# Other orders of moving words in the products of zeros at the head of a recurrence and expert kernel

## The chip, the cores and the metric

The kernel runs on one core of a Trainium2 chip. The metric is device time in microseconds (us); lower is better. The kernel before takes 1058.9 us, the median of three runs (1058.42, 1058.90 and 1058.95).

Engines go by the profile's names: PE is TensorE's matrix products and PEld its loads of held operands (the words that stay in the array while the moving words stream past), DVE is VectorE, ACT is ScalarE, POOL is GpSimd. SP issues most DMAs. L817 is line 817 of the kernel.

## The reference

A gated linear recurrence over 768 steps for 4 batches and 8 heads of 48 values, and then a mixture of 4 experts on the 3072 rows of 384 values that it gives:

```python
for t in range(S):
    state = alpha[:, :, t, :, None] * state + np.einsum('bhd,bhe->bhde', k[:, :, t], v[:, :, t])
    y[:, :, t] = np.einsum('bhd,bhde->bhe', q[:, :, t], state)
x = y.transpose(0, 2, 1, 3).reshape(B * S, H * D)
p = domain_probs / (domain_probs.sum(-1, keepdims=True) + 1e-09)
for e in range(E):
    h = np.maximum(x @ w1[e], 0.0)
    out += p[:, e:e + 1] * (h @ w2[e])
```

Everything is float32. `w1` is 4 x 384 x 1024, `w2` is 4 x 1024 x 384.

## The kernel before

The recurrence is cut into 24 units: one unit is 128 time steps of one batch, all 8 heads. `attention(u)` is a generator; each `next` on it emits one step of one unit's work. The first three steps transpose the unit's alpha, k and q on TensorE (tile tp, L277), and copy or multiply them out of PSUM (L288, L293, L307). Then follow seven levels of doubling (m = 1, 2, 4, ... 64): at each level ScalarE copies every second stretch of m words of q (`copy_q`, qb, L328), VectorE multiplies decays into q and k (`next_q` L335 and L337, `next_k` L348), and TensorE makes the scores (sc, L355; the last level is far, L410). VectorE takes the scores in through masks (`take`, L365), ScalarE and VectorE gather them in lat (L423, L428), and TensorE makes the result (yps, L450), which ScalarE copies into the experts' input xT (L467).

The experts are `up` (the first layer, tiles one and two, L562 and L570) and `down` (the second, tile ops, L663). They go over groups of units: a first group of two, and then groups of four. The first group's first unit, 128 rows, goes through the first expert alone, as soon as its result is there, while the second unit is still on its way.

The order of the work on each engine is the order in which the program emits it (`manual_schedule`); an engine runs its instructions in that order, each one when its operands are there. At the head, which lasts some 30 us, a list written out by hand interleaves steps of units 0 and 1 with products of zeros:

```python
for u, n in ((0, 3), (0, 3), (0, 1), (0, 1), (0, 1), (0, 1), (0, 1), (1, 0), (0, 0), (0, 1),
             (0, 1), (1, 1), (0, 1), (1, 0), (0, 0), (0, 2), (0, 2), (0, 0)):
    next(runs[u])
    (fill if n > 2 else single)(n)
```

After a step of unit `u`, `fill(3)` emits three products of zeros of 128 columns (L798), and `single(n)` emits `n` turns of six products of zeros of 384 columns (L817). The results go to a PSUM tile `idle` that nothing reads; the operands come from `nothing`, a tile of 2304 words a partition that VectorE sets to zero (L794). It is one of the buffers of the first layer's weights, and is free until those need it. Its type is float32r, as that of the experts' products.

There are 13 turns, taken in order from the list `turns`. Turns 1 to 5 stand ahead of the transposes of unit 1's alpha, 6 and 7 ahead of those of its k, 8 and 9 ahead of those of its q, and 10 to 13 ahead of unit 0's result (yps). In the kernel before, a turn is given by four numbers: the step between held words, the step between moving words (negative: backwards), the number of held columns, and where in the tile the moving words begin.

Loads are issued by SP in the order in which they are emitted: inputs of units 0 and 1, the probabilities, four pieces of the first expert's first layer (L221, L222), unit 2's alpha, k and q (L174), and the first expert's second layer (L224).

Of the kernel before, what the change touches and what calls it, by code (L numbers as in the profile page):

```python
# [20 lines left out]
def kernel(  # L21
# [37 lines left out]
    nc = tc.nc  # L59

    B, H, S, D = q.shape
    E, DM, F = moe_w1.shape
    P = 128
# [21 lines left out]
    n = np.arange(QUAD)[None, :]  # L85
# [81 lines left out]
    def load(u, names):  # L167
        if u >= len(units):
            return
        cb, b = units[u]  # L170
        for nm in names:
            src = srcs[nm][b, :, cb * P:(cb + 1) * P, :].rearrange("h s d -> s h d")
            if nm != "v":
                nc.sync.dma_start(out=raw(u, nm)[:, :, :D], in_=src)  # L174
                continue

            pairs = raw(u, nm).rearrange("p (a i) d -> p a i d", i=2)
            src = src.rearrange("p (a i) d -> p a i d", i=2)
            nc.sync.dma_start(out=pairs[:, :, 0, :D], in_=src[:, :, 0])
            nc.sync.dma_start(out=pairs[:, :, 1, :TAIL], in_=src[:, :, 1, QUAD:])  # L180
            nc.sync.dma_start(out=pairs[:, :, 1, TAIL:D], in_=src[:, :, 1, :QUAD])
# [13 lines left out]
    def load_piece(l, i, beside=False):  # L195
        if i >= E * NQ * LAST:
            return
        gi, k = divmod(i, E * NQ)
        e, c = divmod(k, NQ)
        if gi > l:  # L200
            w = wt[l][i] = wts.tile([P, 3, KC * QF], F32R, name=f"w{l + 1}",
                                    bufs=AHEAD if l == 0 else NQ)
            nc.sync.dma_start(out=w.bitcast(F32), in_=kept[l][k])
            return
        if l == 1 and not beside:
            return
        if l == 0:

            if gi > 0 or e == 0:
                shared[c] = wts.tile([P, 3, KC * QF], F32R, name="w2", bufs=NQ)  # L210
            w = shared[c][:, 2 - e % 2 if gi == 0 else 2].bitcast(F32)
        else:

            place = (hidden[c][:, 0] if not split2(gi, e, c) else hidden[c + NQ // 2][:, 1])
            w = place.rearrange("p f n -> p (f n)")[:, :KC * QF].bitcast(F32)
        wt[l][i] = w
        if l == 0:
            heads = moe_w1[e].rearrange("(h d) f -> h d f", d=D)[:, :, c * QF:(c + 1) * QF]
            w = w.rearrange("p (c f) -> p c f", f=QF)
            for part in range(2):  # L220
                nc.sync.dma_start(out=w[:, part], in_=heads[part * H // 2:(part + 1) * H // 2, :QUAD])  # L221
            nc.sync.dma_start(out=w[:, 2], in_=heads[:, QUAD:])  # L222
        else:
            nc.sync.dma_start(  # L224
                out=w.rearrange("p (c d) -> p c d", d=DM),
                in_=moe_w2[e].rearrange("(c p) d -> p c d", p=P)[:, c * FPQ:(c + 1) * FPQ])
# [36 lines left out]
    def norm_probs():  # L263
        nc.vector.reduce_sum(out=tot, in_=p_all, axis=AX.X)
        nc.vector.tensor_scalar_add(out=tot, in0=tot, scalar1=1e-9)
        nc.vector.reciprocal(out=tot, in_=tot)
        nc.vector.tensor_mul(p_all, p_all, tot.unsqueeze(2).broadcast_to([P, NBLK, E]))
        nc.vector.tensor_scalar_mul(out=p_fine, in0=p_all, scalar1=FINE)
# [439 lines left out]
    def cost(layer, gi, e):  # L708
        n = len(groups[gi]) / 4
        if layer == 0:  # L710
            return 2.1 * n if split1(gi, e) else 2.6 * n
        return 4.1 if gi > 1 else 4.7 if split2(gi, e) else 5.4
# [50 lines left out]
    def advance(spent):  # L763
        nonlocal clock
        clock += spent
        while waiting and clock >= waiting[0][0]:
            next(waiting.popleft()[2], None)

    with tc.manual_schedule():
        nc.scalar.dma_start(out=ident_all, in_=nc.inline_tensor(ident_np, name="ident_c").ap())  # L770
        nc.scalar.dma_start(out=masks, in_=nc.inline_tensor(mask_np, name="masks_c").ap())
        nc.gpsimd.memset(sts[B - 1], 0.0)
        for nm in "akq":
            for r in (early[nm], apart[nm]):
                nc.gpsimd.memset(r[:, :, D:], 0.0)
        nc.gpsimd.memset(lat[HALF:, :, :HALF], 0.0)
        for t in values + blocks:
            nc.gpsimd.memset(t, 0.0)
        for t in sts[:-1]:
            nc.gpsimd.memset(t, 0.0)  # L780

        load(0, "akqv")
        load(1, "akqv")
        nc.sync.dma_start(out=p_all, in_=moe_domain_probs.rearrange("(n p) e -> p n e", p=P))
        for i in range(NQ):
            load_piece(0, i)

        idle = ps.tile([P, NT], F32, name="idle", tag="g", bufs=4)  # L790
        zeros = sts[B - 1].rearrange("p a i d -> p (a i d)")[:, :P]
        nothing = wts.tile([P, 3, KC * QF], F32R, name="w1", bufs=AHEAD)
        nothing = nothing.rearrange("p t n -> p (t n)")
        nc.vector.memset(nothing.bitcast(F32), 0.0)  # L794

        def fill(n):
            for _ in range(n):
                nc.tensor.matmul(idle[:, :P], lhsT=zeros, rhs=zeros, start=True, stop=True)  # L798

        def words(n, at):  # L800
            return nothing[:, at:at + n]

        def turn(held=1, moving=1, m=P, away=16):
            return held, moving, m, away

        turns = deque([turn(), turn(2), turn(2, -1), turn(4), turn(4, -1), turn(m=66), turn(1, -1),
                       turn(2, -1, away=12), turn(3), turn(3, -1), turn(1, 2), turn(1, away=20), turn(2, 2)])

        def stepped(n, at, step):
            span = words(n * abs(step), at)[:, ::abs(step)]  # L810
            return span if step > 0 else span[:, ::-1]

        def single(n):
            for _ in range(n):
                held, moving, m, away = turns.popleft()
                for i in range(6):
                    nc.tensor.matmul(idle[:m, :DM], lhsT=stepped(m, 512 * (i % 2), held),  # L817
                                     rhs=stepped(DM, 1024 + away, moving), start=True, stop=True)

        runs = [attention(u) for u in range(len(groups[0]))]  # L820
        fill(7)
# [4 lines that stand above are left out]
        norm_probs()  # L826

        span = cost(0, 0, 0) * FCH / 2 + cost(1, 0, 0)
        waiting.extend((span * (k + 1) / 15, u, runs[u])
                       for k, u in enumerate([1, 1, 1, 0, 1, 0, *[1] * 8]))  # L830
        for fc in range(FCH):
            up(0, 0, fc, slice(0, 1))
            advance(cost(0, 0, 0) / 2)
        down(0, 0, [0], deque())
        while waiting:
            next(waiting.popleft()[2], None)
        clock = 0.0
        waiting.extend((1.0 + k, 1, runs[1]) for k in range(2))
        waiting.extend(deal())

        for (gi, e), after in zip(tasks, [*tasks[1:], (None, None)]):
            rest = gi == e == 0
            for fc in range(FCH):
                up(gi, e, fc, slice(1, len(groups[0])) if rest else None)
                advance(cost(0, gi, e) / (2 if rest else 1))
            each = len(groups[gi]) if split2(gi, e) else 1
            turns = [range(k, k + each) for k in range(rest, len(groups[gi]), each)]
            for k, slots in enumerate(turns):

                between = deque()  # L850
                if after[1] == 0:

                    for step, at in enumerate((0.0, 0.3, 0.42, 0.54) if gi == 0 else
                                              (0.0, 0.6, 0.7, 0.78)):
                        at = at * len(turns) - k
                        if 0 <= at < 1:
                            between.append((at, lambda step=step: split_x(after[0], step)))
                down(gi, e, slots, between)
        while stores:
            stores.popleft()()  # L860
# [28 lines left out]
```

## Time and profile before

| | us |
|---|---|
| median of three runs | 1058.9 |
| the profiled execution | 1059.26 |
| its span, first to last instruction | 1057.4 |
| PE busy (98% of the span) | 1041.3 |
| DVE busy (74%) | 780.9 |
| ACT busy (53%) | 565.7 |
| PE busy in the 78 products of zeros at L817, between 8.15 and 30.03 | 17.5 |

A product's duration in the profile is longer than its share of TensorE's time, because products overlap: one of 384 columns is recorded with some 340 ns, and the next one begins some 174 ns after it. So where the pace matters, the distance from start to start is taken, or a window's length divided by the products in it. In the timeline, instructions of one line that follow each other are put together, with their count; idle time ahead of a row and what ended it stand in brackets.

### The profile page before, as it was taken

How to read it: one execution, taken by the hardware profiler on the slowest of the kernel's cores; microseconds unless marked ns; L12 is line 12 of the kernel's file. 1: busy time of each engine (PE TensorE's matmuls, PEld its weight loads, DVE VectorE, ACT ScalarE, POOL GpSimd, SP SyncE). 2: the span in 40 equal slices, each digit the busy share in tenths (PEclk: the TensorE clock that was granted, in tenths of full speed). 3: DMA queues.
4: the chain of work that ended last, by engine and by line, in shares of the span. 5: the costliest groups of instructions: out<-in, count | busy, mean ns of one | idle time of the engine just before them, and what ended most of it. 6: DMA issues, size and time to landing. Idle time of an engine off the chain costs nothing.

```text
span 1057.4 us, 21736 instructions
## 1 busy us (share of the span) xinstructions
PE 1041.3 (98%) x8560; PEld 905.3 (86%) x8560; DVE 780.9 (74%) x1621; ACT 565.7 (53%) x1195; POOL 37.7 (4%) x81
## 2 busy tenths in 40 slices
PE   9899999999999999999999999999999999999998
PEld 8676777677878798898998998998989889898998
DVE  6477868668778968777877777986978776656565
ACT  4588866664767546446555435555464543323232
POOL 3000000000000100000000000000000000000000
PEclk9999999999999999999999999999999999999999
DMA  7496889897877949568679569586594454444531
GB/s 118 138 301 187 287 264 363 324 349 256 277 254 246 384 133 374 213 211 325 222 231 330 176 256 338 179 304 236 166 370 177 197 209 167 192 179 179 201 158 45
DMA packets 158550, 251.68 MB, mean 238 GB/s; under 512 B 120144, under 2 KB 134864, under 8 KB 135920
## 3 DMA queue, kind: packets, MB, share of 16 engines
q1 hardware_dynamic: 151984, 207.89, 58.4%
q0 software_dynamic: 6016, 42.08, 10.0%
q8 instruction: 68, 1.11, 0.4%
q10 hardware_dynamic: 448, 0.32, 0.1%
q14 instruction: 34, 0.28, 0.1%
HBM read 207.79 MB, written 42.47 MB: 237 GB/s over the span
## 4 chain that ended last, share of the span: by engine, by line
PE 86%; DVE 5%; ACT 5%; DMA 2%; issue 1%; SPq 0%; POOL 0%; ACTq 0%; DVEq 0%; POOLq 0%
PE ops L663 35%; PE one L570 23%; PE two L570 11%; PE sc L355 6%; PE tp L277 3%; PE yps L450 3%; ACT qb L328 2%; PE idle L817 2%; PE one L562 2%; DMA hT<-in_moe_w_dram 1%; PE sps L489 1%; PE far L410 1%; DVE hT L616 1%; DVE near L365 1%; DMA rq<-in_q_dram 1%
## 5 line engine op out<-in xcount | busy, mean ns | idle before, releaser
L663 PE MATMUL ops<-w,hT 128*128 128x384 f32 x1872 | 342.7, 340 | 0.2 <-DVE hT L616 0.2
L663 PEld LDWEIGHTS ops<-w,hT 128*128 128x128 f32 x1872 | 322.6, 188 | 4.0 <-ACT t L581 0.6
L570 PE MATMUL one<-xT,w 128*128 128x512 f32 x960 | 251.9, 398 | 0.4 <-ACT t L581 0.4
L570 PEld LDWEIGHTS one<-xT,w 128*128 128x128 f32 x960 | 176.3, 188 | 38.2 <-ACT t L581 1.2
L581 ACT ACTIVATE t<-one 128x512 f32<-128x512 f32 (+1 forms) x192 | 106.8, 556 | 175.0 <-PE one L570 169.8
L328 ACT COPY qb<-QT 64x256 f32<-64x256 f32 x336 | 136.6, 407 | 58.2 <-DVE QT L335 29.9
L610 DVE SCALAR_TENSOR_TENSOR hT<-t,hT 128x512 fp32r<-128x512 f32 (+1 forms) x172 | 110.4, 642 | 63.3 <-ACT hT L608 62.1
L583 DVE TENSOR_TENSOR t<-t,two 128x512 f32<-128x512 f32 (+1 forms) x172 | 109.3, 635 | 53.2 <-PE two L570 31.7
L608 ACT ACTIVATE hT<-t 128x512 fp32r<-128x512 f32 (+1 forms) x172 | 101.8, 592 | 86.8 <-DVE t L583 86.3
L570 PE MATMUL two<-xT,w 128*128 128x512 f32 x480 | 136.5, 393 | 0.1
L570 PEld LDWEIGHTS two<-xT,w 128*128 128x128 f32 x480 | 90.1, 188 | 20.4 <-DVE acc L692 0.9
L663 PE MATMUL ops<-hT 128*128 128x384 f32 x288 | 100.8, 492 | 0.5 <-DMA hT<-in_moe_w_dram 0.4
L616 DVE SCALAR_TENSOR_TENSOR hT<-hT 128x512 fp32r<-128x512 f32 (+1 forms) x172 | 100.7, 635 | 0.0
L365 DVE COPY_PREDICATED near<-masks,sc 128x256 f32<-128x256 uint8 x144 | 77.1, 536 | 23.3 <-PE sc L355 20.4
L335 DVE TENSOR_TENSOR QT<-QT,dec 128x256 f32<-128x256 f32 x144 | 61.1, 424 | 39.2 <-ACT qb L328 38.6
L355 PEld LDWEIGHTS sc<-qb,KT 128*64 128x64 f32 x2304 | 72.7, 138 | 9.0 <-issue 4.4
L355 PE MATMUL sc<-qb,KT 128*64 128x64 f32 x2304 | 77.2, 223 | 2.6 <-ACT qb L328 2.6
L663 PEld LDWEIGHTS ops<-hT 128*128 128x128 f32 x288 | 52.1, 190 | 30.3 <-DMA hT<-in_moe_w_dram 1.0
L692 DVE SCALAR_TENSOR_TENSOR acc<-ops,p_all,acc 128x384 f32<-128x384 f32 x82 | 49.8, 614 | 27.1 <-PE ops L663 26.3
L348 DVE TENSOR_TENSOR KT<-KT,dec 128x256 f32<-128x256 f32 x144 | 60.3, 419 | 0.0
L347 ACT COPY KT<-KT 128x256 f32<-128x256 f32 x138 | 57.5, 416 | 5.1 <-PE sc L355 1.9
L562 PE MATMUL one<-xT,w 128*128 128x256 f32 (+1 forms) x240 | 46.2, 340 | 0.6 <-ACT xT L467 0.6
(93 smaller groups left out, 949.1 us busy)
## 6 DMA issues: line engine op xcount, KB each, us to landing
w<-kept SPq DMA_DIRECT2D x144, 1152.0 KB
kept<-w POOLq DMA_DIRECT2D x32, 1152.0 KB, 6.9
hT<-in_moe_w_dram SPq DMA_DIRECT2D x32, 384.0 KB
w<-in_moe_w_dram SPq DMA_DIRECT2D x48, 128.0 KB
ra<-in_alpha_dram SPq DMA_DIRECT2D x23, 192.0 KB
rk<-in_k_dram SPq DMA_DIRECT2D x23, 192.0 KB
rq<-in_q_dram SPq DMA_DIRECT2D x23, 192.0 KB
out_dram<-acc POOLq DMA_DIRECT2D x22, 192.0 KB, 6.8
```

Source lines behind the costliest of these rows:

```text
L328: nc.scalar.copy(out=qb[rows, :, i, :].rearrange("p a (b r) -> p a b r", r=m), in_=qv[rows])
L335: nc.vector.tensor_mul(qv, qv, spread(dv[:, :, :, 0], m))
L355: nc.tensor.matmul(out[HALF * s:HALF * (s + 1), 2 * p:2 * p + 2, :], lhsT=KTs[li][:, p, HALF * s:HALF * (s + 1)], rhs=qbs[li][:, p, :, QUA ...
L365: nc.vector.copy_predicated(near.rearrange("p a (b two r) -> p a b two r", two=2, r=m)[:, :, :, 1, :], mk.unsqueeze(1).broadcast_to([P, H, ...
L562: nc.tensor.matmul(one, lhsT=w[:, kc], rhs=xraws[gi][:, kc, lo:hi], start=(kc == 0), stop=(kc == KC - 1))
L570: nc.tensor.matmul(out, lhsT=w[:, part, kc], rhs=x_part(gi, part, kc), start=(part == terms[0] and kc == 0), stop=(part == terms[-1] and k ...
L581: nc.scalar.activation(out=t, in_=one, func=ACT.Copy, scale=FINE)
L583: nc.vector.tensor_add(t, t, two)
L608: nc.scalar.activation(out=top, in_=x, func=ACT.Relu, scale=TRIM)
L610: nc.vector.scalar_tensor_tensor(out=low, in0=x, scalar=0.0, in1=top.bitcast(F32), op0=ALU.max, op1=ALU.subtract)
L616: nc.vector.scalar_tensor_tensor(out=dif, in0=top.bitcast(F32), scalar=1 / 4096.0, in1=low.bitcast(F32), op0=ALU.mult, op1=ALU.subtract)
L663: nc.tensor.matmul(sums[at], lhsT=h, rhs=w, start=(n == begins[at]), stop=(n == ends[at]))
```

## The change

The list of turns is replaced. There are still 13 turns of six products, at the same places, with 384 moving columns each. The held words are now always 128 neighbours. The moving words all begin at word 1040 of the tile. Turn 1 reads 384 neighbours. Turns 2 to 6 read a stretch of 8, 16, 32, 64 and 128 words over and over, turn 7 one of 192 words twice. Turns 8 to 13 read groups of four neighbouring words (a line of 16 bytes): `every(k, n)` takes n groups, each the first of k, and goes over them until 384 words are read. So turns 8 to 11 take every second, fourth, eighth and sixteenth group, turn 12 every third and turn 13 every sixth.

```diff
-        def turn(held=1, moving=1, m=P, away=16):
-            return held, moving, m, away
-
-        turns = deque([turn(), turn(2), turn(2, -1), turn(4), turn(4, -1), turn(m=66), turn(1, -1),
-                       turn(2, -1, away=12), turn(3), turn(3, -1), turn(1, 2), turn(1, away=20), turn(2, 2)])
-
-        def stepped(n, at, step):
-            span = words(n * abs(step), at)[:, ::abs(step)]
-            return span if step > 0 else span[:, ::-1]
+        def again(n):
+            return words(n, 1040).unsqueeze(1).broadcast_to([P, DM // n, n])
+
+        def every(k, n):
+            lines = words(4 * k * n, 1040).rearrange("p (n w) -> p n w", w=4 * k)[:, :, :4]
+            return lines.unsqueeze(1).broadcast_to([P, DM // (4 * n), n, 4])
+
+        turns = deque([words(DM, 1040), *(again(8 << i) for i in range(5)), again(192),
+                       every(2, 48), every(4, 48), every(8, 24), every(16, 12), every(3, 48), every(6, 48)])
 
         def single(n):
             for _ in range(n):
-                held, moving, m, away = turns.popleft()
+                moving = turns.popleft()
                 for i in range(6):
-                    nc.tensor.matmul(idle[:m, :DM], lhsT=stepped(m, 512 * (i % 2), held),
-                                     rhs=stepped(DM, 1024 + away, moving), start=True, stop=True)
+                    nc.tensor.matmul(idle[:, :DM], lhsT=words(P, 512 * (i % 2)), rhs=moving, start=True, stop=True)
```

`words(n, at)` is a stretch of n words of `nothing`.

## The prediction

> **What bounds the kernel now.** I read the page first, for the engine that carries the span; then TensorE's timeline over the first 32 us, where every changed product lies; then the busy time stretch by stretch there; last ScalarE's timeline, for what the products hide. The page:
>
> ```profile
> span 1057.4 us, 21736 instructions
> PE 1041.3 (98%) x8560; PEld 905.3 (86%) x8560; DVE 780.9 (74%) x1621; ACT 565.7 (53%) x1195; POOL 37.7 (4%) x81
> PE ops L663 35%; PE one L570 23%; PE two L570 11%; PE sc L355 6%; PE tp L277 3%; PE yps L450 3%; ACT qb L328 2%; PE idle L817 2%; PE one L562 2%; DMA hT<-in_moe_w_dram 1%; PE sps L489 1%; PE far L410 1%; DVE hT L616 1%; DVE near L365 1%; DMA rq<-in_q_dram 1%
> ```
>
> TensorE is busy 98% of the span, and the products of zeros (idle, L817) hold 2% of the chain that ended last. So they are on the path, and are not filler for a wait. TensorE's timeline says where:
>
> ```profile
> 8.16 6.19 PE L817 MATMUL idle<-w 128*128 128x384 f32 x30
> 14.19 0.60 PE L277 MATMUL tp<-ident,hT 128*128 128x128 f32 x4
> 14.72 2.09 PE L355 MATMUL sc<-qb,KT 128*64 128x64 f32 x64
> 16.73 2.32 PE L817 MATMUL idle<-w 128*66 128x384 f32 x12
> 18.89 0.60 PE L277 MATMUL tp<-ident,hT 128*128 128x128 f32 x4
> 19.24 2.38 PE L817 MATMUL idle<-w 128*128 128x384 f32 x12
> ...
> 23.51 6.59 PE L817 MATMUL idle<-w 128*128 128x384 f32 x24
> 30.03 1.08 PE L450 MATMUL yps<-lat,rv 128*32 128x128 f32 x32
> 31.71 3.62 PE L562 MATMUL one<-xT,w 128*128 128x128 f32 x30 [0.60 <-ACT xT L467]
> ```
>
> Columns: start, length, engine, line, count, and idle time before. From 8.16 to 31.11 us no row has idle time: each real step stands behind a run of zero products, and moves when they get longer or shorter. The same stretches by turn (six products each), L817 alone; the counts include a neighbour that reaches over an edge:
>
> ```profile
> 8.15:11.38 3.23, 3.22 (x18) 3.23 (x19) 1.00 1.54 161
> 11.38:14.19 2.81, 2.81 (x13) 2.71 (x12) 1.00 1.00 50
> 16.72:18.89 2.17, 2.16 (x12) 1.81 (x12) 1.00 0.38 109
> 19.23:21.47 2.24, 2.23 (x12) 2.13 (x12) 1.00 0.26 92
> 23.50:24.72 1.22, 1.21 (x6) 1.21 (x7) 1.00 0.32 109
> 24.73:26.77 2.04, 2.04 (x7) 1.24 (x7) 1.00 0.51 155
> 26.77:27.84 1.07, 1.07 (x7) 1.06 (x6) 1.00 0.70 172
> 27.84:30.03 2.19, 2.19 (x7) 1.07 (x6) 1.00 0.64 144
> ```
>
> First column: window and its length; then TensorE and weight loads; the granted clock is 1.00 in all. Three prices are to be read. A plain turn costs 1.04 to 1.07 us (start to start 0.174 us a product, from the single instructions; the first after other work 0.1 to 0.17 more). Turns 4 and 5, whose held words are four apart, cost 2.81 for two: 0.234 a product, with weight loads of 330 ns for the usual 188 to 195. Turns 11 and 13, whose moving words are two apart, cost 2.04 and 2.19: 0.345 a product, twice the plain one. Backward moving words (turns 3, 7, 8), held words two or three apart and 66 columns cost nothing over a plain turn (0.174 to 0.177).
>
> **The change, part by part.** It removes no product and adds none: 78 before, 78 after, in the same places, 384 moving columns each. No DMA, wait or instruction on another engine changes, and none is moved past another on any queue; only TensorE's pace does.
>
> Held words become 128 neighbours everywhere. Turns 4 and 5 then cost 12 x 0.174 = 2.09 and the way out, some 2.11, instead of 2.81: **0.70 us saved** ahead of the transposes at 14.19. Turn 6 goes from 66 columns to 128 at no price: both have 0.174, since a weight load of 188 ns overlaps the product before it; without that cover it would be 6 x 0.05 = 0.3 us.
>
> Turns 11 and 13 lose the step of two: if their new orders run at 0.174 they cost 1.05 and about 1.14 (with the way out), **0.99 + 1.05 = 2.04 us saved** ahead of the yps products.
>
> New orders. Seven turns are one stretch of 384 words, or 8 to 192 words repeated; six take four neighbouring words from every second, fourth, eighth, sixteenth, third and sixth group of four. No row of before moves words so into TensorE, so I bound them. From below, 0.1725: the 48 products of 384 words in one piece of L663 take 8.33 us in the chain (0.1735 each), and no row of that type moves a word faster than 0.45 ns; a gain beyond 78 x 0.001 us = 0.1 us is excluded. From above, 0.345 for words two apart, if a jump over a group costs what that jump did, and four times 0.174 = 0.69 if the cost follows the words jumped over up to sixteen.
>
> Which is nearer? The trace lets the unit of a read be worked out. Held words one, two, three and four apart load in 188, 190 to 195, 252 and 330 ns. If reads came in units of two words, three apart would cost as much as four apart; so a unit has at least four. Against a larger one stands ScalarE's copy at L328: 256 words a partition at every level, taken as one of two (level 0), two of four (level 1), four of eight (level 2), eight of sixteen and so on; over the 48 copies of each level the medians are 424 and 422 ns, then 402, 403, 402, 402 and 402. The same rows in the timeline:
>
> ```profile
> 9.30 0.85 ACT L328 COPY qb<-QT 64x256 f32<-64x256 f32 x2 [1.38 <-DVE QT L307]
> 10.71 0.87 ACT L328 COPY qb<-QT 64x256 f32<-64x256 f32 x2 [0.55 <-DVE QT L335]
> 12.20 0.82 ACT L328 COPY qb<-QT 64x256 f32<-64x256 f32 x2 [0.62 <-DVE QT L335]
> ...
> 19.58 0.59 ACT L293 COPY KT<-tp 128x512 f32<-128x512 f32 x1 [0.97 <-PE tp L277]
> ```
>
> Half-used groups of four cost 20 ns; whole groups with every second left out cost nothing. With a unit of eight words level 2 would use half of each and cost the 20 ns too. So the unit is four, one is read in about 1.8 ns (345 ns / 192 at step two, 174 / 96 at step one, 0.2335 us / 128 for held words four apart), and the new six turns use every one they touch whole: 96 per product, as one stretch of 384 does. I take **0.174 for all 78** and keep 0.1725 and 0.69 for the range. It is an inference from another engine's port, so not certain.
>
> The Trainium skill, SBUF — State Buffer, Specifications (TRN2), also names 16-byte lines and asks for at least two hits on a line for full bandwidth. Turns 11 and 13 have two hits a line and run at half pace, so for moving words the measurement decides against that number. By the page alone they would already be at full pace, nothing would be had there, and the sum would be the 0.70 of the held words: an estimate of 1058.2.
>
> What is late next. After turn 5 the transposes of the second unit start at 13.48; their input's wait was passed in TensorE's queue at 10.35. ScalarE's copy of them gains less (0.42), as ScalarE is in the level-3 copy until 14.40, but the 64 score products behind need that copy only for their last 16, 1.5 us on. So they end 0.7 earlier, and so do turns 6 and 7, and the transposes at 18.89, for which ScalarE waits (0.97 us in the row above). Its level-6 copy and the far products follow 0.7 earlier. VectorE's mask work must be 0.34 earlier for that, and has 0.39 to give in its own wait for scores at 15.92. After turn 13, yps moves from 30.03 to about 27.3; its last input, lat, was ready at 25.32 and will be at 24.6, so TensorE still sets that place. Behind it, xT, the 128-column products from 31.71 and the second unit hang on TensorE and ScalarE. The weights for the first expert's second layer, issued from 30.50 to 32.65 behind a full DMA queue, don't move; they land by 36.8 and are wanted at 42.03, now 39.3. Cover is left; without it the gain would be lost there.
>
> **Sum:** 0.70 + 2.04 = 2.74 us off the profiled execution's 1059.26 (span 1057.4 and 1.86 around it): 1056.5. That execution is 0.36 above the median of the runs, so 1058.9 - 2.7 = **1056.2**.
>
> **The rivals.**
> *Absorbed.* Between 132 and 160 us the chain runs through DMAs (a q load of 6.72 us, then expert weights for 12.12). If these started by the clock, 2.7 us gained before would be waited off there: 1056.8 to 1058.9. Against: each is issued after ScalarE work (131.95 and 147.32) that moves as well, and TensorE's wait for them is 0.2 and 0.36 us.
>
> *Runs cost something.* The new orders have 96 runs in each of 36 products and 2 to 48 in the repeated ones: some 4000 runs. At 0.25 to 0.6 ns each they give back 1.0 to 2.4 us: 1057.2 to 1058.6. Against: ScalarE's 64 runs at level 2 cost no more than 4 at level 6.
>
> *Other side: jumps over groups double the product,* in turns 8 to 13, as a unit larger than four words on TensorE's port would make it. 36 products at 0.345: turns 8 and 9 +2.05 us, the last gap 24 x 0.345 + 0.1 = 8.4 against 6.52, +1.9, less 0.70: +3.2, so 1062.1. It decides from 0.250 us a product on (0.174 + 2.74 / 36). If only even jumps double (two banks), turn 12 is spared: 1061.1. If cost follows the words jumped over to sixteen: turns 8 and 12 at 0.345 and 0.52, the other four at 0.69, about +12.4: 1071.
>
> *The orders are not what reaches the array,* for instance folded into one stretch: then all run at 0.174 as well, and the time is that of the forecast.
>
> **How the numbers follow.** Full pace that reaches the end: 0.66, its own range 1055.4 to 1056.8 (the 0.1 us from below, run-to-run 0.5, a loss of up to 0.6). Absorbed 0.11; runs cost 0.09; doubled 0.09; fourfold 0.05. A measurement of this kernel tells about 0.2%, 2.1 us, from no change. Faster by more is the first case, 0.66; the next two lie within, 0.20; the last two are slower, 0.14. The range reaches up to the spared-turn case, 1061.1, and leaves out the rest of the slower ones and the tail below 1055.4.
>
> **What would show it.** The windows of turns 4 and 5 together at about 2.1 us, of turns 11 and 13 at about 1.05 and 1.1; all L817 products near 340 ns and no weight load of 330; yps at about 27.3 with still no idle row before it; everything after earlier by 2.7, first at 160 us and then at the end. Wrong would be: products of turns 8 to 13 longer than 0.18 apart, idle time ahead of yps, or a DMA wait of 2 us or more before 200 us.

## The result and the profile after

The changed kernel takes 1056.69 us (median of 15 runs, 1056.17 to 1057.64); the kernel before, run beside it, 1059.02 (15 runs). The ratio is 0.9976 with a 95% interval of 0.9968 to 0.9984, that is 1.7 to 3.4 us saved. The forecast was 1056.2, with a range of 1055.4 to 1061.1. So it went the way that was forecast and nearly as far; but two steps of the working were off, in opposite directions: the new orders do not all run at one pace, and one of them is faster than the prediction thought possible.

The page of the changed kernel (span, busy time and the chain that ended last):

```profile
span 1055.1 us, 21736 instructions
PE 1038.8 (98%) x8560; PEld 904.0 (86%) x8560; DVE 780.8 (74%) x1621; ACT 566.0 (54%) x1195; POOL 37.8 (4%) x81
PE ops L663 35%; PE one L570 23%; PE two L570 11%; PE sc L355 5%; PE tp L277 3%; PE yps L450 3%; ACT qb L328 2%; PE idle L817 1%; PE one L562 1%; PE sps L489 1%; DMA hT<-in_moe_w_dram 1%; PE far L410 1%; DMA ra<-in_alpha_dram 1%; SPq L221 1
```

The span is 2.3 us shorter, TensorE's busy time 2.5 us, its weight loads 1.3 us; the other engines' busy times differ by 0.3 us at most. TensorE's timeline at the head (start, length, line, count, idle time before):

```profile
5.45 1.11 PE L798 MATMUL idle<-st 128*128 128x128 f32 x6
...
7.86 5.47 PE L817 MATMUL idle<-w 128*128 128x384 f32 x30
13.18 0.60 PE L277 MATMUL tp<-ident,hT 128*128 128x128 f32 x4
13.71 2.08 PE L355 MATMUL sc<-qb,KT 128*64 128x64 f32 x64
15.72 2.35 PE L817 MATMUL idle<-w 128*128 128x384 f32 x12
17.91 0.60 PE L277 MATMUL tp<-ident,hT 128*128 128x128 f32 x4
18.26 2.37 PE L817 MATMUL idle<-w 128*128 128x384 f32 x12
...
22.52 5.21 PE L817 MATMUL idle<-w 128*128 128x384 f32 x24
27.66 1.08 PE L450 MATMUL yps<-lat,rv 128*32 128x128 f32 x32
29.34 3.62 PE L562 MATMUL one<-xT,w 128*128 128x128 f32 x30 [0.60 <-ACT xT L467]
```

Still no idle time in the gaps, and the same 0.60 us ahead of L562 as before: nothing else became late. From the first product at L817 to the transposes behind turn 5 it is 5.31 us, before 6.03: 0.72 us saved. The last gap, up to yps, is 5.14 us, before 6.52: 1.38 saved. The yps products start 2.37 us earlier, and matmul by matmul the two traces then stay some 2.4 us apart to 140 us, 2.16 from 160 to 169 us, and 2.25 to 2.30 from 171 us to the end.

0.72 and 1.38 don't make 2.37; the turns between gave back 0.03, and the other 0.30 is there before the first changed product: the six products at L798 take 1.11 us, in the kernel before 1.43.

```profile
5.43 1.43 PE L798 MATMUL idle<-st 128*128 128x128 f32 x6
```

That is the same code in both. In the profiled execution of before, the trace records the full granted clock from 6.7 us after the start, in this one from 6.0 us. Up to that point the products at L798 begin 0.21 us apart, and behind it 0.11 us. Over the executions profiled below, which share these first products, the point lies between 4.6 and 7.3 us. It is luck of the one execution and no part of the change. So the change itself is worth some 2.0 to 2.1 us at the head, and not the 2.74 of the sum.

Where the rest went shows turn by turn. These windows hold turns 1 to 3 and 8 to 13 of the changed kernel, instructions of the tile idle alone (window, its length, busy time of TensorE and of weight loads with their counts, granted clock, DMA share, GB/s; the counts take in neighbours that reach over an edge):

```profile
7.86:8.99 1.13, 1.13 (x6) 1.13 (x7) 1.00 1.53 165
8.99:9.98 0.99, 0.99 (x7) 0.99 (x7) 1.00 1.54 164
9.98:11.07 1.09, 1.09 (x8) 1.09 (x7) 1.00 1.53 161
...
18.26:19.38 1.12, 1.12 (x6) 1.12 (x7) 1.00 0.35 110
19.39:20.46 1.07, 1.07 (x7) 0.91 (x6) 1.00 0.25 90
22.52:23.76 1.24, 1.24 (x6) 1.23 (x7) 1.00 0.31 109
23.77:25.06 1.29, 1.29 (x7) 1.18 (x7) 1.00 0.45 144
25.07:26.11 1.04, 1.04 (x7) 1.03 (x6) 1.00 0.94 229
26.12:27.65 1.53, 1.53 (x7) 0.99 (x6) 1.00 0.30 99
```

The first, and those of turns 8 and 10 (18.26 and 22.52), begin behind other work and hold some 0.1 us more for that. The second is eight words repeated: 0.99 us, 0.165 a product, **faster** than one stretch. The last four are every eighth, sixteenth, third and sixth group. From start to start, in the middle of each turn, a product takes 0.193, 0.217, 0.174 and 0.240 us. Not the distance, then: third is free and sixth is the dearest, and sixteenth is cheaper than sixth.

### The profile page after: what moved, and what is told of

The parts are those of the page before. It is cut to its first block, busy times and chain, and to the rows that moved or that the text cites. A ratio compares the mean times of both kernels' runs of the same rounds, so it can differ in the third digit from the quotient of the medians.

```text
span 1055.1 us, 21736 instructions
## 1 busy us (share of the span) xinstructions
PE 1038.8 (98%) x8560; PEld 904.0 (86%) x8560; DVE 780.8 (74%) x1621; ACT 566.0 (54%) x1195; POOL 37.8 (4%) x81
## 3 DMA queue, kind: packets, MB, share of 16 engines
q8 instruction: 68, 1.11, 0.4%
## 4 chain that ended last, share of the span: by engine, by line
PE 85%; ACT 4%; DVE 4%; DMA 3%; SPq 1%; issue 1%; POOL 0%; ACTq 0%; DVEq 0%; POOLq 0%
PE ops L663 35%; PE one L570 23%; PE two L570 11%; PE sc L355 5%; PE tp L277 3%; PE yps L450 3%; ACT qb L328 2%; PE idle L817 1%; PE one L562 1%; PE sps L489 1%; DMA hT<-in_moe_w_dram 1%; PE far L410 1%; DMA ra<-in_alpha_dram 1%; SPq L221 1%; DMA rq<-in_q_dram 1%
## 5 line engine op out<-in xcount | busy, mean ns | idle before, releaser
L570 PE MATMUL one<-xT,w 128*128 128x512 f32 x960 | 251.8, 398 | 0.4 <-ACT t L581 0.4
L570 PEld LDWEIGHTS one<-xT,w 128*128 128x128 f32 x960 | 176.2, 188 | 38.1 <-ACT t L581 1.2
L570 PE MATMUL two<-xT,w 128*128 128x512 f32 x480 | 136.5, 393 | 0.1
L570 PEld LDWEIGHTS two<-xT,w 128*128 128x128 f32 x480 | 90.0, 188 | 20.5 <-DVE acc L692 0.9
L562 PE MATMUL one<-xT,w 128*128 128x256 f32 (+1 forms) x240 | 46.2, 340 | 0.6 <-ACT xT L467 0.6
```

The costliest lines, as they stand in the source:

```text
L570: nc.tensor.matmul(out, lhsT=w[:, part, kc], rhs=x_part(gi, part, kc), start=(part == terms[0] and kc == 0), stop=(part == terms[-1] and k ...
```

## The experiments

**Is it the order, or the place in the timeline?** The slow turns all stand between 22 and 28 us. Reversing the list moves them to the front.

```diff
-                       every(2, 48), every(4, 48), every(8, 24), every(16, 12), every(3, 48), every(6, 48)])
+                       every(2, 48), every(4, 48), every(8, 24), every(16, 12), every(3, 48), every(6, 48)][::-1])
```

> The same thirteen orders, last turn first. If the pace belongs to the order (theory), the order of every sixth group, now turn 1, stays at 0.240 us a product, every sixteenth (turn 3) at 0.217, every eighth (turn 4) at 0.192, eight words repeated (turn 12) at 0.165, and the last gap, now 64, 32, 16 and 8 words repeated and one stretch less one, shrinks to some 4.3 us; the gains change places and the time stays within 0.3 us of the changed kernel's. If the pace belongs to the place in the timeline (rival: what other engines and DMAs do from 22 to 28 us), turn 1 runs at 0.174 and the last two or three turns at 0.19 to 0.24.

The order carries its pace with it. Windows of every sixth, sixteenth and eighth group near the front, and of eight words repeated in the last gap:

```profile
7.97:9.46 1.49, 1.49 (x6) 1.27 (x7) 1.00 1.53 164
10.53:11.80 1.27, 1.27 (x7) 1.15 (x7) 1.00 1.46 140
11.82:12.94 1.12, 1.12 (x7) 1.12 (x6) 1.00 0.99 42
...
25.57:26.54 0.97, 0.97 (x7) 0.97 (x7) 1.00 0.65 166
```

A product is at 0.240, 0.216, 0.188 and 0.165 us. The last gap fell to 4.38 us, as expected. But the end did not follow. This execution took 1059.1 us, the kernel before beside it 1058.55. At 169 us it was still 2.36 us ahead of before; it lost 2.0 us of that in one wait, ahead of the first products of a later group (timeline), and the rest by 200 us:

```profile
170.25 1.62 PE L570 MATMUL one<-xT,w 128*128 128x512 f32 x6 [1.88 <-DVE near L365]
```

The profile names VectorE. But the semaphore updates in the trace show the last part of this group's first piece of weights (w<-kept, issued at L203) landing at 170.11 us, 0.14 us ahead of the product. The same 0.13 to 0.14 us lies between the two in all twelve traces of this case: 170.46 and 170.60 us in the kernel before, 168.16 and 168.30 in the changed one. So this DMA sets the start, and did so in the kernel before, where no row shows a wait. Here it landed late: from 150 to 155 us the DMAs moved 306 GB/s, where the changed kernel's execution has 420 (last column; this run first):

```profile
150.00:155.00 5.00, 5.00 (x24) 4.39 (x24) 3.98 (x9) 4.77 (x13) 0.00 (x0) 1.00 1.00 306
```

```profile
150.00:155.00 5.00, 5.00 (x24) 4.22 (x23) 4.54 (x10) 4.79 (x11) 0.00 (x0) 1.00 1.05 420
```

That is the rival "absorbed", in one execution and at another place than the prediction gave it. Whether it comes with the kernel or by chance of an execution, more executions of the same list tell:

> The reversed list of turns once more, in rounds. Its profile was 2.34 us ahead of the kernel before up to 169 us and then gave all of it back in one wait of 1.9 us for expert weights, while the DMAs moved 306 GB/s from 150 to 155 us instead of 405 to 420. If that was chance of one execution (theory), its median lies 2.0 to 2.6 us under the kernel before, as the changed kernel's. If the new phase of the head against the DMAs does it (rival), the median lies within 0.8 us of the kernel before.

1056.96 us (median of 10 runs, 1055.62 to 1058.04), ratio 0.998 (0.997 to 0.9989). None of the ten reaches 1059.1, and the profiled one has the wait at 168 us at 0.38 us. So the kernel does not bring that loss with it; an execution may pay it or not. What sets it was not tested. A single execution of this kernel is good for the pace of its products, and not for a microsecond of its time.

**Both parts apart.** The kernel before, with neighbours as held words throughout, and its own moving orders.

```diff
-                    nc.tensor.matmul(idle[:m, :DM], lhsT=stepped(m, 512 * (i % 2), held),
+                    nc.tensor.matmul(idle[:m, :DM], lhsT=stepped(m, 512 * (i % 2), 1),
```

> The kernel before with held words always neighbours, and its own moving orders: one part of the change alone. Turns 4 and 5 fall from 0.234 to 0.174 us a product and the distance from the first product at L817 to the transposes behind turn 5 from 6.03 to 5.33 us; turns 11 and 13 stay at 0.345 and the last gap at 6.5 us. The end comes 0.70 us earlier, give or take what the clock's start in the first 8 us does (0.3). If held words four apart had been hidden, nothing moves.

Turns 4 and 5 together, then turns 11 and 13, in windows:

```profile
11.06:13.17 2.11, 2.11 (x13) 1.95 (x12) 1.00 1.09 71
23.61:25.64 2.03, 2.03 (x7) 1.24 (x7) 1.00 0.44 139
26.73:28.86 2.13, 2.13 (x7) 1.02 (x6) 1.00 0.61 158
```

2.11 us was the prediction's figure for the first; the other two stand as before. From the first product at L817 to the transposes it is 5.34 us, 0.69 less. The end lies 0.73 us ahead in the trace, but that it equals the 0.70 expected is partly luck: the yps products were 1.16 us ahead, 0.33 of it from before the first product at L817, and 0.43 of that lead was lost by the end, behind a wait of 0.72 us for the weights near 170 us. The one execution took 1058.43 us, the kernel before beside it 1058.55; the times alone would not tell 0.7 us from nothing. The other part alone, every product with the one stretch:

```diff
-        turns = deque([words(DM, 1040), *(again(8 << i) for i in range(5)), again(192),
-                       every(2, 48), every(4, 48), every(8, 24), every(16, 12), every(3, 48), every(6, 48)])
+        turns = deque([words(DM, 1040) for _ in range(13)])
```

> All 78 products read the one stretch of 384 words from word 1040: the sum of the prediction without the new orders. Theory: 0.174 us a product in all turns, the last gap at 4.45 us instead of the changed kernel's 5.14, unit 0's result 0.75 us earlier against the first product at L817 (19.05 us behind it instead of 19.79): the missing part of the predicted 2.04 us is the price of every 6th, 8th and 16th group and nothing else. If the last gap's place costs something by itself (rival), some turns there stand above 0.18 and the gap at 4.7 to 5.1.

```profile
22.92 4.44 PE L816 MATMUL idle<-w 128*128 128x384 f32 x24
27.29 1.08 PE L450 MATMUL yps<-lat,rv 128*32 128x128 f32 x32
```

All turns at 0.172 to 0.174, the gap 4.37 us, and yps 18.96 us behind the first product, against 19.79 in the changed kernel and 21.87 in the kernel before. The sum of the prediction, 2.74, is near for these plain orders (2.91 from the first product on). The changed kernel has the same held words and places, so the 0.83 us between the two is the price of the new moving orders, taken together. The one execution took 1056.55 us, the kernel before beside it 1058.50.

**What makes an order slow?** First, a clash with the loads of held words, which read the same tile at the same time. With 66 held columns they read half as much:

```diff
-                    nc.tensor.matmul(idle[:, :DM], lhsT=words(P, 512 * (i % 2)), rhs=moving, start=True, stop=True)
+                    nc.tensor.matmul(idle[:66, :DM], lhsT=words(66, 512 * (i % 2)), rhs=moving, start=True, stop=True)
```

> The changed kernel's moving orders with 66 held columns instead of 128 in every product of zeros at L817, so that the loads of held words read half as much. If the slow orders lose their time to a clash of the two reads in the same memory (theory), every sixth, sixteenth and eighth group get faster: half of the extra 0.066, 0.043 and 0.018 us a product goes, 0.207, 0.195 and 0.183. If the moving reads alone set it (rival), they stay at 0.240, 0.217 and 0.192 within 0.004.

Windows of turns 10, 11 and 13 (every eighth, sixteenth and sixth group):

```profile
22.11:23.35 1.24, 1.24 (x6) 0.90 (x7) 1.00 0.32 111
23.37:24.64 1.27, 1.27 (x7) 0.86 (x6) 1.00 0.37 131
25.70:27.21 1.51, 1.51 (x7) 0.72 (x5) 1.00 0.54 146
```

They are at 0.205, 0.215 and 0.241 us a product: none got faster by more than 0.003, though a load of held words fell from some 190 ns to 140. So a clash that grows with the held words read falls. Every eighth got slower, which no theory here expected, and it stays unexplained. (The execution took 1056.03 us.)

Next, the distance, the jumps back at the end of a pass, or the steps themselves:

```diff
+        turns = deque([words(DM, 1040), every(5, 48), every(6, 24), every(6, 48, 0), every(7, 32), every(8, 48, 0),
+                       every(12, 24), every(10, 24), every(32, 12, 0), every(16, 24, 0), every(3, 96), every(6, 48),
+                       every(6, 96, 0)])
```

> Other steps, starts and counts, one turn each: one stretch, every 5th group, every 6th with half as many groups (gone over four times instead of twice), every 6th from word 0, every 7th, every 8th without a repeat of its 24 groups (48 groups), 12th, 10th, 32nd, 16th with 24 groups, every 3rd with 96 groups, every 6th as in the change, every 6th with 96 groups. If the cost grows with the distance jumped (theory A), 5th lies between 3rd and 6th and 7th to 32nd at 0.24 or more. If it comes from the jumps back at the end of a pass (theory B), every 6th with 96 groups (no jump back) is at 0.174, with 24 groups above 0.30, and every 32nd (8 passes) is the slowest. If it comes from certain steps falling on few banks (theory C), even steps cost and odd ones (5th, 7th) run at 0.174 to 0.177, wherever they begin.

Windows of turns 2 to 5 (every 5th, 6th in four passes, 6th from word 0, 7th), 11 (3rd in one pass) and 13 (6th in one pass, with the way out to the yps products):

```profile
8.73:9.90 1.17, 1.17 (x7) 1.13 (x7) 1.00 1.54 163
9.92:11.34 1.42, 1.42 (x7) 1.19 (x6) 1.00 1.54 160
11.36:12.78 1.42, 1.42 (x7) 1.19 (x6) 1.00 1.26 71
12.80:13.87 1.07, 1.07 (x7) 0.91 (x5) 1.00 1.19 25
...
25.05:26.07 1.02, 1.02 (x7) 1.02 (x6) 1.00 0.67 190
...
27.52:29.04 1.52, 1.52 (x7) 0.99 (x5) 1.00 0.48 133
```

Distance falls: 7th and 12th are at 0.178, 6th at 0.240. Jumps back fall: the sixth is at 0.240 in one, two or four passes, and from either start. And "odd steps are free" falls, since the fifth is at 0.200. 8th is at 0.193, 10th at 0.189, 16th and 32nd both at 0.217. (This execution took 1062.89 us. 2.89 us of it are the wait ahead of L570, here with the DMA of expert weights named. Behind that wait the granted clock was 0.50 for 3.4 us, and the nine products there ran at half pace, 0.427 us apart for 0.23, which cost another 1.6 us. The wait of 1.88 us above had no such row.)

```profile
172.93:176.35 3.42, 3.42 (x10) 2.58 (x9) 0.35 (x1) 0.60 (x1) 1.08 (x2) 0.50 0.99 415
```

That 16 and 32 cost the same suggested a pattern that comes back. First, more orders, and whether the four words of a line are what is paid for:

```diff
+        turns = deque([again(4), again(2), again(8, 1041), words(DM, 1041), every(2, 48, 1042), every(4, 96),
+                       every(5, 96), every(9, 48), every(11, 48), every(12, 48), every(14, 32), every(20, 24),
+                       every(24, 24)])
```

Here `every` starts at word 0 unless a start is given.

> More orders, one turn each: four words over and over, two words, eight words from word 1041 (off the groups of four), one stretch from 1041, every 2nd group from 1042 (each group across two lines), every 4th with 96 groups, 5th with 96, 9th, 11th, 12th, 14th, 20th and 24th. If a product cannot go below 384 array cycles (theory), four and two words stay at 0.160 to 0.166. Groups across two lines read twice as many lines: 0.30 to 0.345 if lines are what is paid for, 0.174 if only words are. 4th and 5th with 96 groups keep 0.178 and 0.200. If few banks make the slow steps, the odd 9 and 11 are at 0.172 to 0.200 and 20 and 24 near the 0.189 to 0.192 of 8 and 10; if distance did, all from 9 on lie above 0.19.

Windows of two words repeated, one stretch from word 1041, and every second group from word 1042:

```profile
8.55:9.52 0.97, 0.97 (x7) 0.97 (x7) 1.00 1.54 163
10.54:11.56 1.02, 1.02 (x7) 1.02 (x7) 1.00 1.56 155
11.58:13.60 2.02, 2.02 (x7) 1.02 (x6) 1.00 1.13 46
```

A group of four words that lies across two lines doubles the product, 0.345 us against 0.173 for the same order from word 1040. Units of two words would have cost the same from both starts, and with units of eight every second group would have cost twice the one stretch; so lines of four words are what is paid for. Two, four or eight words over and over run at 0.165 to 0.166, even eight that touch three lines (word 1041); that is as low as any order here goes. Why is not shown: that lines just read cost nothing would fit these, but sixteen words over and over, four lines, are at 0.181 in the changed kernel. 9th is at 0.173, 11th 0.177, 12th 0.181, 14th 0.178, 20th 0.178, and 24th at 0.189 as the 8th. With 4 = 20, 8 = 24 and 16 = 32, a period of sixteen groups, 256 bytes, was the guess, and it gives a number for steps that had not run:

```diff
+        turns = deque([every(17, 32), every(18, 32), every(21, 24), every(22, 24), every(23, 24), every(26, 16),
+                       every(27, 16), every(30, 16), every(37, 12), every(38, 12), every(40, 12), every(48, 12),
+                       every(64, 8)])
```

> Steps of 17, 18, 21, 22, 23, 26, 27, 30, 37, 38, 40, 48 and 64 groups, one turn each. If the pace has a period of sixteen groups (256 bytes; theory), each has the price of its remainder: 17 as 1 (0.174), 18 as 2 (0.173), 21 and 37 as 5 (0.200), 22 and 38 as 6 (0.240), 23 as 7 (0.178), 26 as 10 (0.189), 27 as 11 (0.176), 30 as 14 (0.178), 40 as 8 (0.189 to 0.193), 48 and 64 as 16 (0.217). If every long step costs (rival), all are at 0.19 to 0.24 with no such order; if only 5, 6 and multiples of sixteen as such cost, 21, 22, 37 and 38 are at 0.174 to 0.18.

Windows of the 21st, 22nd, 23rd and 48th:

```profile
10.37:11.49 1.12, 1.12 (x7) 1.12 (x7) 1.00 1.55 155
11.51:12.92 1.41, 1.41 (x7) 1.19 (x7) 1.00 1.22 58
12.94:14.03 1.09, 1.09 (x7) 0.93 (x5) 1.00 1.01 23
...
26.06:27.33 1.27, 1.27 (x7) 1.17 (x7) 1.00 0.87 213
```

us a product, from start to start in the middle of each turn, by the step's remainder:

| remainder of 16 | steps run: us a product |
|---|---|
| 1 | 1: 0.174; 17: 0.175 |
| 2 | 2: 0.173; 18: 0.174 |
| 5 | 5: 0.200; 21: 0.190; 37: 0.184 |
| 6 | 6: 0.240; 22: 0.240; 38: 0.220 |
| 7 | 7: 0.178; 23: 0.180 |
| 8 | 8: 0.193; 24: 0.189; 40: 0.187 |
| 10 | 10: 0.189; 26: 0.189 |
| 11 | 11: 0.177; 27: 0.176 |
| 14 | 14: 0.178; 30: 0.177 |
| 0 | 16: 0.217; 32: 0.217; 48: 0.217; 64: 0.213 |

The period holds in the main: 22 groups apart is as dear as six, and 23 apart as cheap as seven. The rivals (all long steps cost; five and six as such) fall. It is not exact: the fifth's relatives are cheaper than expected, 0.190 and 0.184 for 0.200, and the 38th is at 0.220. These have 24 and 12 lines a pass, against 48. For every sixth group 24 lines a pass changed nothing (0.240), and no run has 12, or 24 for the fifth. What stands behind the period, banks of the memory or something else, was not tested, and why remainder 6 costs more than 0 stays open. (The execution took 1058.04 us.)

**A version that beats both.** Eight words over and over being the fastest order of the change, all products can read them:

```diff
+        turns = deque([again(8) for _ in range(13)])
```

> All 78 products read the same eight words over and over, the fastest order of the change (0.165 us a product). Each is at 0.165 to 0.166, the last gap falls from 5.14 to 4.2 us, and the result of unit 0 starts 1.4 us earlier than in the changed kernel, near 26.3 us. If the gain reaches the end (theory), the median is 1.4 us under the changed kernel's, some 1055.3. If the DMAs from 140 to 172 us have no more to give (rival), it stays at 1056 to 1056.7.

The last gap, and the first products behind the DMA wait:

```profile
22.26 4.22 PE L816 MATMUL idle<-w 128*128 128x384 f32 x24
26.41 1.08 PE L450 MATMUL yps<-lat,rv 128*32 128x128 f32 x32
...
167.82 1.62 PE L570 MATMUL one<-xT,w 128*128 128x512 f32 x6 [1.05 <-DMA w<-kept]
```

All turns run at 0.164 to 0.166; yps starts 18.26 us behind the first product, 1.53 less than in the changed kernel. The median is 1055.66 us (8 runs, 1055.28 to 1058.38), ratio to the kernel before 0.9971 (0.9961 to 0.9981). By the medians 1.0 of the 1.5 us reaches the end: 1055.66 lies between the theory's 1055.3 and the rival's 1056 to 1056.7. The profiled execution was 3.62 us ahead of before at yps and 2.78 behind the wait at 167 us, so it left 0.84 us there. And since the last gap's products held up a result whose inputs were there, twelve of them can go (this one leaves out products that nothing reads):

```diff
-                     (0, 1), (1, 1), (0, 1), (1, 0), (0, 0), (0, 2), (0, 2), (0, 0)):
+                     (0, 1), (1, 1), (0, 1), (1, 0), (0, 0), (0, 1), (0, 1), (0, 0)):
```

> As all-eight-words, and the last gap has two turns instead of four: 12 products less. The result of unit 0 then waits for its lat copies instead of for the products of zeros and starts at 24.2 to 24.6 us, 3.2 us earlier than in the changed kernel. If all of it reaches the end, the median is some 1053.3. If the DMA wait near 170 us takes the place of the products removed (rival), 1054.5 to 1056. If the granted clock falls in the gap: 1056 or more.

Timeline, VectorE's lat copy and TensorE:

```profile
22.02 2.25 PE L816 MATMUL idle<-w 128*128 128x384 f32 x12
...
23.38 0.42 DVE L428 COPY lat<-near 64x512 f32<-64x512 f32 x1
...
24.19 1.08 PE L450 MATMUL yps<-lat,rv 128*32 128x128 f32 x32
```

**1053.62 us** (median of 5 runs, 1052.97 to 1055.95), ratio 0.9953 (0.9939 to 0.9966): 5.5 us under the kernel before by the medians (1059.15 beside it), and 2.0 under all-eight-words. yps starts at 24.19 us as expected, though still behind products of zeros: lat was there at 23.80, so at 0.165 us each an estimated two products more could go; that was not run. In the profiled execution no DMA wait took the place of the removed work: ahead of L570 it is 0.22 us.

## Why the prediction was right, and where it was not

- *What bounds the head.* Right: TensorE's unbroken run of zero products; each microsecond less there arrived at yps, and the 0.60 us idle ahead of L562 did not grow. What the account of "what is late next" missed lies further on: the weights whose landing sets the start of L570 at 170.60 us in the kernel before. The changed kernel's profiled execution lost only 0.1 us there, because they landed 2.30 us earlier; for these weights the prediction had not worked that out.
- *Held words, 0.70 us.* Right: 0.72 in the change, 0.69 alone.
- *Moving words, 2.04 us.* Mis-sized: 1.38. The step that failed is the price of the new orders, "I take 0.174 for all 78". Right for every second and third group and nearly for every fourth (0.178); wrong for every eighth, sixteenth and sixth: 0.193, 0.217 and 0.240. Six of each at 0.019, 0.043 and 0.066 more is 0.77 us. Plain orders would have saved 2.15 in the last gap, 6.52 to 4.37 in the run of one stretch; less 0.77 that is the measured 1.38. Products of turns 8 to 13 longer than 0.18 us apart are a sign of being wrong that the prediction itself named, and it came true in turns 10, 11 and 13.
- *The bound from below.* Failed: "a gain beyond 78 x 0.001 us = 0.1 us is excluded". Eight words repeated run at 0.165, 0.009 less, and all 78 so take 0.7 us off the plain order from the first product to yps (18.96 to 18.26). No row of before re-read its lines, so none could exclude it.
- *The unit of a read is four words.* Right, by a route over weight loads and another engine's copies. But from "the new six turns use every one they touch whole" it does not follow that any choice of lines costs the same: ScalarE's rows leave out every second stretch and nothing else, at a slower pace (402 ns for 256 words).
- *The rivals.* Doubling jumps: no, the dearest order is 0.240, and the point given from which it decides, 0.250 for all 36, was not neared on average (0.196). "Two banks": no, the even steps of two and four cost little or nothing (0.173 and 0.178), and the odd fifth costs 0.200. (For cost that follows the words jumped over, its own terms give +12.7, not +12.4; 0.69 was not neared.) Folded into one stretch: no, since the orders differ in pace. Runs that cost something: no, 96 runs in one pass of every third group are at 0.173. Absorbed: of little weight in the median, but real in single executions, up to 2.9 us, at 168 to 172 us rather than before 160.
- *The number.* 1056.2 against 1056.69, or 2.7 us saved against 2.33. The traces give 2.0 to 2.1 at the head, less some 0.1 left at the DMAs; in the profiled pair luck with the clock puts 0.3 on top. The interval of the runs, 1.7 to 3.4, holds both 2.0 and 2.7, so that the number came out so near says little about the working.

## What to carry to other kernels

Work that is there only to keep an engine busy must be costed like any other: look whether the real step behind it had its inputs already, and cut it to that. Price an access order by a row with the same order on the same port; a row from another engine gives the unit, not the pace. And where one wait on a saturated DMA may cost two microseconds or nothing, read a change's effect from its own stretch, and its time from many runs.

## What the runs showed of the hardware

All rows are of products of zeros in float32r, 384 moving columns, at a granted clock of 1.00 except where said.

- Moving words of 4 bytes are paid for in lines of 16 bytes: a stretch of 384 neighbours costs 0.174 us from word 1040 or 1041, every second line used whole the same, and lines of which half is used twice that (0.345).
- A pattern with a period of sixteen lines lies over it: steps of 6 and 22 lines cost 0.240 (38: 0.220), multiples of 16 0.213 to 0.217, 5 and 21 0.200 and 0.190, 8, 10, 24, 26 and 40 0.187 to 0.193, the others run 0.173 to 0.184. The 0.240 of every sixth line does not hang on start, place, passes or held columns; every eighth line went from 0.193 to 0.205 with 66 held columns.
- Up to eight words read over and over are faster than one stretch: 0.165 against 0.174; sixteen are slower, 0.181. The cause is open.
- Held words four apart cost 0.234 a product; with neighbours, 66 and 128 held columns cost the same in plain orders (0.174).
- After 2.89 us without a product (the run of other steps) the granted clock was 0.50 for 3.4 us; after 1.88 us (the reversed list) it stayed at 1.00.
